# Two PSUM banks as two tensors instead of one, and V and w_in laid out by even and odd columns, in a fused attention and feed-forward kernel

## The chip, the core and the metric

The kernel runs on one core of a Trainium2 chip. A core has a matrix engine (PE in the profile, with its weight loads listed apart as PEld), a vector engine (DVE), a scalar engine (ACT), a general engine (POOL) and a queue engine (SP). Each works through its own list of instructions in order and waits on semaphores for the others. Matmul results go to PSUM, which has eight banks of 2 KB in each of 128 partitions; a bank holds 512 float32 values. The metric is device time in microseconds. The kernel before took 403.68 us, the median of three runs (402.3, 403.68 and 404.91).

## The reference, cut to what matters

Attention of 8 x 8 heads over 576 tokens with head dimension 64. A token sees the tokens within 32 of it; 8 global tokens see all and are seen by all. Its output, 4608 tokens of 512 features, goes through a feed-forward layer with weights w_in (512 x 2048) and w_out (2048 x 512).

```
scores = 0.125 * q @ k.T                          # per batch and head
mask   = (|i - j| <= 32) or i is global or j is global
attn   = softmax(where(mask, scores, -1e9))
x      = (attn @ v) as [4608 tokens, 8 heads * 64]
h      = x @ w_in
out    = (s * relu(h)**2 + b) @ w_out
```

## The kernel before, in words

Work on attention goes by pairs of heads: 32 pairs, four to a batch. For pair p the keys are cut in five chunks. `qk(p, c)` (L517) is one matmul of up to 384 columns into a tile `pss`, an exponential on ACT into `e` (L523), and a multiplication with the mask on DVE into `em` (L526). After every second pair `pvq` (L528) multiplies `em` by V, four heads side by side, each in its own 32 columns of the array. The stationary operand is a 32-column piece of `vring`, where V lies in bf16; `part` 0 is a column of ones for the sums, `part` 1 and 2 are the first and the second half of a head's 64 columns. Two steps of the normalisation follow (L590, L593) and DVE writes x, transposed, into `xt`, whose four slices of 128 partitions are pairs of heads and halves of their columns. The rows of `w_in` must lie in the same order; L164 and the four loads at L837 do that. Eight copies on POOL (L608, `scatter`) put the global tokens' columns into `xt` when a batch is done.

The feed-forward layer goes by tiles of 512 tokens, nine in all, 32 quanta each (`moe_quanta`, L616). Quantum f of the first 16 takes a bank, runs four matmuls of 512 columns over w_in into it (L631), and ACT evicts it with a ReLU into `r` (L638), which DVE squares into `g` (L641). The last 16 quanta are four banks of 16 matmuls over w_out (L650), which DVE evicts as `osb` or `osbh` (L670, L667). Each time a bank is taken is a turn; `bank` (L106) counts them.

Of the eight banks `ps_s` (for `pss` and some transposes) takes two, `ps_o` (for `po`) two, `ps_m` two, and `ps_x` holds one tile of two banks, named `spare` in the code and `psx` in the profile. In the first pairs `spare` is a second accumulator for `pvq` (blocks with `blk` 1, `m` below 2), and the place that the warming matmuls on zeros (`warm`, L780) write. After pair 4 `early` is false, and `bank` hands out in turn two tiles of `ps_m` (named `psh`, `pso`, `pst`, `psg`), then the first half of `spare`, then its second half, and so on: two turns in `ps_m`, two in `spare`. Whatever is written or read there is then named `psx`.

The order of every engine's instructions is the order of the code (a manual schedule); `later` holds steps that are put behind the next matmuls. Pairs 0 to 4 run alone (`first_pair`); from pair 5 on each of a pair's eight steps (`run_pair`) has one quantum of the feed-forward layer behind it, so that from about 50 us on the two kinds of work alternate, and from about 330 us on the last tiles run alone. The queue of POOL carries in order: the loads of k and q of pairs 1 to 3 (`load_kq`, L170, rounding to bf16 on the way), the gathers of the global rows, two of the four w_in loads, k and q of pair 4, the other two w_in loads, a cast of V, V of pair 4, and so on.

Of the kernel before, what the change touches and what calls it, by code (L numbers as in the profile page):

```python
# [9 lines left out]
FP32 = mybir.dt.float32  # L10
# [6 lines left out]
P = 128  # L17
# [3 lines left out]
DM, DF = 512, 2048  # L21
# [16 lines left out]
NVR = 5  # L38
# [7 lines left out]
DH = D // 2  # L46
# [13 lines left out]
def view(ap, *dims):  # L60

    return bass.AP(
        tensor=ap.tensor, offset=ap.offset, ap=[list(ap.ap[0])] + [list(d) for d in dims]
    )
# [3 lines left out]
def kernel(  # L68
# [12 lines left out]
    nc = tc.nc  # L81
# [15 lines left out]
    globp = ctx.enter_context(tc.tile_pool(name="globp", bufs=2))  # L97
    ps_s = ctx.enter_context(tc.tile_pool(name="ps_s", bufs=2, space=bass.MemoryType.PSUM))
    ps_o = ctx.enter_context(tc.tile_pool(name="ps_o", bufs=1, space=bass.MemoryType.PSUM))
    ps_x = ctx.enter_context(tc.tile_pool(name="ps_x", bufs=1, space=bass.MemoryType.PSUM))  # L100
    ps_m = ctx.enter_context(tc.tile_pool(name="ps_m", bufs=2, space=bass.MemoryType.PSUM))
    spare = ps_x.tile([P, 2 * DM], FP32, tag="x", name="psx")
    turns = [0]
    early = [True]

    def bank(name):  # L106

        turns[0] += 1
        if early[0] or turns[0] % 4 < 2:
            return ps_m.tile([P, DM], FP32, tag="moe", name=name)[:]  # L110
        return spare[:, DM * (turns[0] % 2) :][:, 0:DM]


    from concourse.hw_specs import get_activation_tables
# [25 lines left out]
    for t, eng in (("k", nc.sync), ("q", nc.scalar)):  # L140
        eng.dma_start(
            out=six0[t].rearrange("p (h x) -> p h x", h=2),
            in_=src[t][0, 0:2].rearrange("h (p j) d -> p h (j d)", j=NJ),
# [5 lines left out]
        out=gidx_p[:],  # L149
        in_=bass.AP(  # L150
            tensor=global_idx.tensor, offset=global_idx.offset, ap=[[0, P // NG], [1, NG], [1, 1]]
        ),
    )
    nc.scalar.dma_start(out=gidx_i64[:], in_=_bcast_dram(global_idx[:], P))
    vring = const.tile([P, NVR, NCH, 2, D], BF16)
    qbufs = [const.tile([P, 2, LQ], BF16, name=f"qbd{i}", tag=f"qbd{i}") for i in range(3)]
    gqd = [const.tile([P, 2, D], BF16, name=f"gqd{i}", tag=f"gqd{i}") for i in range(2)]
    win_t = wpool.tile([P, 4, DF], BF16)
# [2 lines left out]
    wsum = wpool.tile([P, DM], FP32)  # L161
    s_bc = const.tile([P, 1], FP32)
    b_bc = const.tile([P, 1], FP32)
    w_in2 = moe_w_in.rearrange("(g j h i) f -> j i g h f", g=2, j=4, h=2)  # L164
    w_out2 = moe_w_out.rearrange("(a p) n -> p a n", p=P)

    def load_kq(p):
        bi, hp = divmod(p, 4)
        for t in "kq":
            nc.gpsimd.dma_start(  # L170
                out=six[t][:NP6, p % NR].rearrange("p h j d -> p h (j d)"),
                in_=src[t][bi, 2 * hp : 2 * hp + 2].rearrange("h (p j) d -> p h (j d)", j=NJ),
            )
# [69 lines left out]
    def cast_v(eng, p):  # L243
# [4 lines left out]
            name=nc.get_next_instruction_name(), act_func_set_id=_set_id,  # L248
# [18 lines left out]
    for t in gqd:  # L267
# [21 lines left out]
    part = const.tile([P, 1], I32)  # L289
    nc.vector.tensor_scalar(  # L290
        out=part[:], in0=rowi[:], scalar1=3, scalar2=7,
# [5 lines left out]
        out=half[:], in0=partf[:], scalar=2.0 * S, in1=half[:], op0=OP.mult, op1=OP.add  # L297
    )
    nc.vector.tensor_copy(
        out=six["k"][:NP6, 0].rearrange("p h j d -> p (h j d)"), in_=six0["k"]  # L300
# [48 lines left out]
    for t in gadd:  # L349
# [7 lines left out]
        out=band[:], in0=band[:], scalar1=(float(WIN) + 0.5) ** 2, scalar2=None, op0=OP.is_le  # L357
# [25 lines left out]
    def flush():  # L383
        ops, later[:] = list(later), []
        for f in ops:
            f()

    def globals_of(bb):
# [9 lines left out]
        def turn():  # L398
            ps = bank("psg").bitcast(BF16)[:, 0 : 2 * D].rearrange("p (i d) -> p i d", i=2)
            for i in range(2):  # L400
                for hh in range(2):
                    r = slice(D * hh, D * hh + D)
                    nc.tensor.transpose(ps[r, i], gb[r, i], ident[r, r])

            def evac():
                eng = nc.vector.tensor_copy if bb else nc.scalar.copy
                eng(out=gkt[bb][:], in_=ps[:, 0])
                for hh in range(2):
                    r = slice(D * hh, D * hh + D)
                    eng(out=gqd[bb % 2][r, hh], in_=ps[r, 1])  # L410

            later.append(evac)
# [115 lines left out]
    def pvq(m, blk):  # L528

        po = spare if blk and m < 2 else ps_o.tile([P, 2 * DM], FP32, tag="o", name="po")  # L530
        otile[(m, blk)] = po
        x0, x1 = SPAN[blk]
        started = set()
        for part in range(3):
            for c in range(NCH):
                lo, hi = max(LO[c], x0), min(HI[c], x1)
                while lo < hi:
                    a = CUT * part + lo - x0
                    n = min(hi - lo, DM * (a // DM + 1) - a)
                    for j in range(4):  # L540
                        p, hh = 2 * m + j // 2, j % 2
                        key = (a // DM, j)
                        nc.tensor.matmul(  # L543
                            po[DH * j : DH * j + DH, a : a + n],
                            vring[:, p % NVR, c, hh, DH * (part - 1) : DH * part]
                            if part
                            else onesb[:],
                            emt[(p, c)][:, hh, lo - LO[c] : lo - LO[c] + n],
                            start=key not in started, stop=(part == 2),
                            skip_group_check=True,  # L550
                        )
                        started.add(key)
                    lo += n
# [127 lines left out]
    moe = moe_quanta()  # L681
# [18 lines left out]
    def put_out(m, blk):  # L700
        pvq(m, blk)
        pending.extend(norm_steps(m, blk))
# [48 lines left out]
            Q(nq[s])  # L751

    def idle_bank():
        return spare[:, 0:DM] if early[0] else bank("psw")

    def select(p):

# [22 lines left out]
    def warm(n):  # L780

        ps = idle_bank()
        for _ in range(n):
            nc.tensor.matmul(ps, dummy[:, 0:P], dummy[:])  # L784

    def first_pair(p, extra={}):
# [40 lines left out]
        out=sel6[:], in0=view(idx6[:], [1, NJ], [0, NG]),  # L827
# [5 lines left out]

    gather(0, "kqv")
    load_kq(3)
    for a in range(4):
        nc.gpsimd.dma_start(  # L837
            out=win_t[:, a], in_=w_in2[:, :, a // 2, a % 2]
        )
        if a == 1:  # L840
            load_kq(4)
    clear(qbufs[1][0:D, 1], LQ)
    clear(qbufs[1][D:P, 0], LQ)
# [5 lines left out]
        out=vkey[:], in0=kidx[:], scalar1=float(S) - 0.5, scalar2=None, op0=OP.is_le  # L849
    )  # L850
    for i in range(2):
        c = i * (NCH - 1)
        nc.vector.tensor_copy(
            out=gadd[i][:, GAP : GAP + NG], in_=view(vkey[:, c : c + 1], [0, NG])
# [3 lines left out]
        out=sel[:], in0=view(kidx[:], [1, NCH], [0, NG]),  # L858
# [42 lines left out]
        elif p == 2:  # L901
            load_kq(6)
    flush()
    early[0] = False
    warm(12)
    scatter(0)
    load_w_out(1)
# [1 line left out]
    for i in (1, 2, 3):  # L909
# [5 lines left out]
        out=view(natb[96:P], [DM, NV * NCH * P // DM], [1, DM]),  # L915
        in_=view(dummy[96:P], [0, NV * NCH * P // DM], [1, DM]),
    )
    nc.sync.dma_start(
        out=view(six["q"][96:P], [384, 10], [1, 384]), in_=view(dummy[96:P], [0, 10], [1, 384])
# [28 lines left out]
    for p in range(4, NPAIR):  # L948
# [18 lines left out]
        if p == 5:  # L967
            for i in range(NG):
                nc.gpsimd.dma_start(
                    out=gvall[i : i + 1].rearrange("o (b h d) -> o b h d", b=B - 2, h=H),  # L970
                    in_=v[2:, :, ds(greg_p[i], 1), :].rearrange("b h o d -> o b h d"),
# [6 lines left out]
        if p >= 6 and p + 2 < NPAIR:  # L978
# [4 lines left out]
            for i, j in enumerate(todo):  # L983
                if j < NPAIR:
                    x = 4 if p in (8, 9) else 4 * i
# [66 lines left out]
```

## Time and profile before

| | |
|---|---|
| median of three runs | 403.68 us |
| profiled execution: time, span of the core | 407.0 us, 405.3 us |
| PE busy | 352.4 us, 87% of the span, 3232 matmuls |
| DVE, ACT, POOL busy | 238.4, 226.1, 72.1 us |
| mean granted PE clock | 0.966 |
| ACT's evictions `r` from `psx`, from `psh` | 74 and 70 |
| HBM read, written | 42.20 MB, 9.44 MB |

The profile is of one execution, whose time is 3.3 us above the median. Times in rows count from the span's start. A row of the timeline gives start, length, engine, line, operation, output and input, and in brackets how long the engine stood idle before and what ended that. Matmuls overlap in the pipeline: a row's length of a lone matmul of 512 columns is longer than the step from one to the next.

### The profile page before, as it was taken

To read this page: it belongs to the slowest core of one execution; us is meant where nothing else is said; L and a number is where in the kernel's file an instruction comes from. 1 tells how busy PE (TensorE), PEld (TensorE's weight loads), DVE (VectorE), ACT (ScalarE), POOL (GpSimd) and SP (SyncE) were. 2 spreads that over 40 slices of the span, in tenths; PEclk is the share of its full clock that TensorE was granted. 3 is DMA by queue.
4 is the path that set the end of the run, shared out by engine and by line. 5 is a ranking of instruction groups with operands and counts; after the bars stand their busy time and mean duration, and the time that the engine had idled before them with its cause. 6 is when DMAs were issued, how large, how long until landed. Compare 5 with 4: busy or idle time off the path is not lost.

```text
span 405.3 us, 8660 instructions
## 1 busy us (share of the span) xinstructions
PE 352.4 (87%) x3232; PEld 178.0 (44%) x3232; DVE 238.4 (59%) x677; ACT 226.1 (56%) x454; POOL 72.1 (18%) x151
## 2 busy tenths in 40 slices
PE   7773889898999799988988889898989898899896
PEld 3341444454444244556643434344446543344344
DVE  6663656866868379776665566766665643322421
ACT  6661657655885377756773676667656623502510
POOL 7824484206001201050002000300020010000000
PEclk9995798999999699999998999999999999999999
DMA  6999799999979677859157924882430011011002
GB/s 133 180 154 151 117 173 224 173 188 229 179 133 196 120 179 146 212 116 193 46 136 190 221 62 121 203 184 45 137 96 29 2 53 53 2 53 53 0 27 78
DMA packets 122197, 50.51 MB, mean 125 GB/s; under 512 B 108819, under 2 KB 115635, under 8 KB 122155
## 3 DMA queue, kind: packets, MB, share of 16 engines
q1 hardware_dynamic: 112058, 37.49, 43.4%
q0 software_dynamic: 9600, 12.04, 17.0%
q8 instruction: 25, 0.41, 0.4%
q10 hardware_dynamic: 496, 0.43, 0.4%
q14 instruction: 18, 0.14, 0.1%
HBM read 42.20 MB, written 9.44 MB: 127 GB/s over the span
## 4 chain that ended last, share of the span: by engine, by line
issue 40%; PE 37%; POOL 6%; DMA 5%; ACT 5%; DVE 4%; SPq 1%; POOLq 0%; ACTq 0%
PE psx L631 9%; PE psh L631 8%; PE pso L650 7%; PE psx L650 7%; DMA sixq<-in_q_dram 5%; ACT r L638 3%; POOL xt L608 3%; PE po L543 2%; PE pss L519 2%; POOL gf L319 2%; PE psx L784 1%; PE pst L472 1%; DVE xt L584 1%; POOL vring L244 1%; DVE osb L670 1%
## 5 line engine op out<-in xcount | busy, mean ns | idle before, releaser
L523 ACT ACTIVATE e<-pss 128x384 bf16<-128x384 f32 (+1 forms) x160 | 74.5, 470 | 55.6 <-PE pss L519 52.3
L631 PEld LDWEIGHTS <-win_t 128*128 128x128 bf16 x704 | 65.1, 99 | 87.6 <-issue 38.3
L641 DVE TENSOR_TENSOR g<-r 128x512 bf16<-128x512 bf16 x144 | 59.8, 422 | 67.5 <-ACT r L638 65.5
L631 PE MATMUL psx<-xt,win_t 128*128 128x512 bf16 (+2 forms) x364 | 77.9, 345 | 23.9 <-ACT r L638 20.5
L650 PEld LDWEIGHTS <-g 128*128 128x128 bf16 x592 | 56.5, 98 | 67.3 <-issue 10.0
L650 PE MATMUL pso<-wout_t,g 128*128 128x512 bf16 (+1 forms) x320 | 73.6, 369 | 0.0
L631 PE MATMUL psh<-xt,win_t 128*128 128x512 bf16 (+2 forms) x340 | 72.2, 349 | 1.5 <-POOL xt L608 1.5
L526 DVE TENSOR_TENSOR em<-e,mask 128x384 bf16<-128x384 bf16 (+1 forms) x160 | 55.8, 349 | 30.1 <-ACT e L523 29.9
L638 ACT ACTIVATE r<-psx 128x512 bf16<-128x512 f32 x74 | 44.4, 600 | 50.4 <-PE psx L631 45.5
L650 PE MATMUL psx<-wout_t,g 128*128 128x512 bf16 x272 | 66.6, 387 | 6.5 <-DVE osb L670 6.0
L638 ACT ACTIVATE r<-psh 128x512 bf16<-128x512 f32 x70 | 42.0, 599 | 41.5 <-PE psh L631 40.4
L519 PE MATMUL pss<-qbd,kt 128*128 128x384 bf16 (+1 forms) x160 | 53.0, 340 | 2.8 <-DVE qbd L447 1.6
L608 POOL COPY xt<-xg 128x4 bf16 x64 | 17.3, 270 | 167.9 <-DVE xt L584 164.4
L519 PEld LDWEIGHTS <-kt 128*128 128x128 bf16 x160 | 16.1, 102 | 21.7 <-DVE qbd L447 4.1
L584 DVE TENSOR_TENSOR xt<-po,rep 128x120 bf16<-128x120 f32 (+1 forms) x60 | 25.1, 459 | 0.5 <-ACT rep L594 0.5
L501 DVE COPY qbd<-pst 64x600 bf16<-64x600 bf16 x38 | 17.8, 468 | 11.6 <-PE pst L459 11.1
L506 DVE COPY qbd<-pst 64x600 bf16<-64x600 bf16 x20 | 15.6, 778 | 14.1 <-ACT qbd L506 8.1
L670 DVE SCALAR_TENSOR_TENSOR osb<-psx,s_bc,bias_row 128x512 f32<-128x512 f32 x12 | 9.0, 746 | 18.3 <-PE psx L650 18.3
L543 PE MATMUL po<-em,vring 128*32 128x160 bf16 (+2 forms) x896 | 18.3, 221 | 0.1
L201 ACT CAST natb<-natk 120x640 bf16<-120x640 f32 x24 | 17.4, 726 | 0.0
L784 PE MATMUL psx<-dummy 128*128 128x512 bf16 x33 | 14.0, 535 | 3.4 <-DVE xt L584 2.0
L929 POOL DMA_DIRECT2D wst<-in_moe_w_out_dram x8 | 5.8, 731 | 60.7 <-DVE wsum L933 34.2
(121 smaller groups left out, 289.2 us busy)
## 6 DMA issues: line engine op xcount, KB each, us to landing
natv<-in_v_dram SPq DMA_DIRECT2D x55, 150.0 KB
natk<-in_k_dram SPq DMA_DIRECT2D x47, 150.0 KB
out_dram<-osb SPq DMA_DIRECT2D x23, 256.0 KB
natq<-in_q_dram SPq DMA_DIRECT2D x37, 150.0 KB
wst<-in_moe_w_out_dram POOLq DMA_DIRECT2D x8, 512.0 KB, 5.2
out_dram<-osbh SPq DMA_DIRECT2D x9, 256.0 KB
win_t<-in_moe_w_in_dram POOLq DMA_DIRECT2D x4, 512.0 KB, 19.7
wout_t<-in_moe_w_out_dram POOLq DMA_DIRECT2D x4, 512.0 KB, 9.1
```

What stands on the lines that cost most here:

```text
L501: eng(out=view(qbufs[p % 3][r, hh], [P, NCH], [HB + NG, 2], [1, HB]), in_=view(ps[r], [P, NCH], [HB, 2], [1, HB]),)
L519: nc.tensor.matmul(ps[:], ktile[p][:, P * c : P * c + P], qbufs[p % 3][:, :, LO[c] : HI[c]])
L523: nc.scalar.activation(e[:], ps[:], AF.Exp, scale=SCALE)
L526: later.append(lambda: nc.vector.tensor_mul(em[:], e[:], masks[c]))
L543: nc.tensor.matmul(po[DH * j : DH * j + DH, a : a + n], vring[:, p % NVR, c, hh, DH * (part - 1) : DH * part] if part else onesb[:], emt[( ...
L584: nc.vector.tensor_tensor(out=view(xt[:, 2 * g, x0 + t0 :], [NXT, 2], [w, runs], [1, w]), in0=view(po[:, CUT + col :], [CUT, 2], [P, runs] ...
L608: nc.gpsimd.tensor_copy(out=xt[:, :, S * (bi % NX) : S * (bi % NX) + S][:, :, ds(greg_p[i], 1)], in_=xgs[bi][:, :, i : i + 1],)
L631: nc.tensor.matmul(psh[:, d0 : d0 + n], win_t[:, a, f * P : f * P + P], xt[:, a, x0 : x0 + n], start=(a == 0 and j == 0), stop=(a == 3), s ...
L638: nc.scalar.activation(r[:], psh, AF.Relu)
L641: later.append(lambda g=g, r=r: nc.vector.tensor_mul(g[:], r[:], r[:]))
L650: nc.tensor.matmul(pso[:, 0:nn], gl[f][:, u * P : u * P + P], wout_t[:, f, n0 : n0 + nn], start=(f == 0), stop=(f == 15),)
L784: nc.tensor.matmul(ps, dummy[:, 0:P], dummy[:])
```

## The change

Three edits. First, `ps_x` with its tile `spare` is opened in a stack of its own, which is closed after pair 4, and a pool `ps_n` with two one-bank tiles takes its place; `bank` takes two turns from `ps_m`, then two from `ps_n`. The turn numbers and so the banks stay the same, but each turn's tile is now a tensor of its own. Second, `part` 1 and 2 of V are the even and the odd columns of a head, so that the stationary operand is read with a step of two elements. Third, `w_in` is ordered to match: partition p of slice (g, h) holds row 256 g + 2 p + h, so a partition's two rows for one g lie side by side in memory. The four loads are now by halves of the 2048 columns (outer) and by g (inner), each of 128 partitions x 2 rows x 1024 columns, where each was one slice of 128 partitions x 2048 columns. The pair-4 load stays between the second and the third.

```diff
--- before.py
+++ after.py
@@ -97,18 +97,18 @@
     globp = ctx.enter_context(tc.tile_pool(name="globp", bufs=2))
     ps_s = ctx.enter_context(tc.tile_pool(name="ps_s", bufs=2, space=bass.MemoryType.PSUM))
     ps_o = ctx.enter_context(tc.tile_pool(name="ps_o", bufs=1, space=bass.MemoryType.PSUM))
-    ps_x = ctx.enter_context(tc.tile_pool(name="ps_x", bufs=1, space=bass.MemoryType.PSUM))
     ps_m = ctx.enter_context(tc.tile_pool(name="ps_m", bufs=2, space=bass.MemoryType.PSUM))
+    first = ctx.enter_context(ExitStack())
+    ps_x = first.enter_context(tc.tile_pool(name="ps_x", bufs=1, space=bass.MemoryType.PSUM))
     spare = ps_x.tile([P, 2 * DM], FP32, tag="x", name="psx")
     turns = [0]
-    early = [True]
+    rings = [ps_m]
 
     def bank(name):
 
         turns[0] += 1
-        if early[0] or turns[0] % 4 < 2:
-            return ps_m.tile([P, DM], FP32, tag="moe", name=name)[:]
-        return spare[:, DM * (turns[0] % 2) :][:, 0:DM]
+        pool = rings[turns[0] // 2 % len(rings)]
+        return pool.tile([P, DM], FP32, tag="moe", name=name)[:]
 
 
     from concourse.hw_specs import get_activation_tables
@@ -161,7 +161,7 @@
     wsum = wpool.tile([P, DM], FP32)
     s_bc = const.tile([P, 1], FP32)
     b_bc = const.tile([P, 1], FP32)
-    w_in2 = moe_w_in.rearrange("(g j h i) f -> j i g h f", g=2, j=4, h=2)
+    w_in2 = moe_w_in.rearrange("(g p h) f -> p g h f", g=2, h=2)
     w_out2 = moe_w_out.rearrange("(a p) n -> p a n", p=P)
 
     def load_kq(p):
@@ -542,7 +542,7 @@
                         key = (a // DM, j)
                         nc.tensor.matmul(
                             po[DH * j : DH * j + DH, a : a + n],
-                            vring[:, p % NVR, c, hh, DH * (part - 1) : DH * part]
+                            view(vring[:, p % NVR, c, hh, part - 1 :], [2, DH])
                             if part
                             else onesb[:],
                             emt[(p, c)][:, hh, lo - LO[c] : lo - LO[c] + n],
@@ -751,7 +751,7 @@
             Q(nq[s])
 
     def idle_bank():
-        return spare[:, 0:DM] if early[0] else bank("psw")
+        return spare[:, 0:DM] if len(rings) == 1 else bank("psw")
 
     def select(p):
 
@@ -833,11 +833,11 @@
 
     gather(0, "kqv")
     load_kq(3)
-    for a in range(4):
-        nc.gpsimd.dma_start(
-            out=win_t[:, a], in_=w_in2[:, :, a // 2, a % 2]
-        )
-        if a == 1:
+    for j in range(2):
+        x = slice(1024 * j, 1024 * j + 1024)
+        for g in range(2):
+            nc.gpsimd.dma_start(out=win_t[:, 2 * g : 2 * g + 2, x], in_=w_in2[:, g, :, x])
+        if j == 0:
             load_kq(4)
     clear(qbufs[1][0:D, 1], LQ)
     clear(qbufs[1][D:P, 0], LQ)
@@ -901,7 +901,8 @@
         elif p == 2:
             load_kq(6)
     flush()
-    early[0] = False
+    first.close()
+    rings.append(ctx.enter_context(tc.tile_pool(name="ps_n", bufs=2, space=bass.MemoryType.PSUM)))
     warm(12)
     scatter(0)
     load_w_out(1)
```

On every engine the instructions stand in the same order as before; names of tiles, waits and the shape of the four loads differ.

PE, the first quanta of tile 7, in the last stage without attention, before (`psx_102` is `spare`; a number after a name is one tensor):

```order
L631 MATMUL psx_102<-xt_108,win_t_122 128x512
L631 LDWEIGHTS win_t_122
L631 MATMUL psx_102<-xt_108,win_t_122 128x512 [waits Activation_49]
...
L631 LDWEIGHTS win_t_122
L631 MATMUL psh_5688<-xt_108,win_t_122 128x512
...
L631 MATMUL psx_102<-xt_108,win_t_122 128x512 [waits Activation_49]
...
L631 MATMUL psx_102<-xt_108,win_t_122 128x512 [waits Activation_49]
```

And the same places now:

```order
L631 MATMUL psh_5741<-xt_108,win_t_122 128x512
L631 LDWEIGHTS win_t_122
L631 MATMUL psh_5750<-xt_108,win_t_122 128x512 [waits DVE_49]
...
L631 LDWEIGHTS win_t_122
L631 MATMUL psh_5768<-xt_108,win_t_122 128x512 [waits Activation_49]
...
L631 MATMUL psh_5777<-xt_108,win_t_122 128x512 [waits Activation_49]
...
L631 MATMUL psh_5786<-xt_108,win_t_122 128x512 [waits Activation_49]
```

No matmul moved. Before, all turns in `spare` write one tensor, and the wait of the third row is for ACT's read of the other half, which the matmuls directly ahead of it have just filled. Now every turn has its own tensor, and the wait at a turn's first matmul is for the reader of the same bank four turns back.

POOL, the loads around w_in, as one piece of the difference:

```order
 L170 DMA sixk<-in_k_dram 96x2x384
 L170 DMA sixq<-in_q_dram 96x2x384 [waits DMASW0_49]
-L837 DMA win_t<-in_moe_w_in_dram 128x1x2048 [waits DMASW1_49]
-L837 DMA win_t<-in_moe_w_in_dram 128x1x2048 [waits DMASW2_49]
+L839 DMA win_t<-in_moe_w_in_dram 128x2x1024 [waits DMASW1_49]
+L839 DMA win_t<-in_moe_w_in_dram 128x2x1024 [waits DMASW2_49]
 L170 DMA sixk<-in_k_dram 96x2x384 [waits DMASW3_49]
 L170 DMA sixq<-in_q_dram 96x2x384 [waits DMASW4_49]
-L837 DMA win_t<-in_moe_w_in_dram 128x1x2048 [waits DMASW5_49]
-L837 DMA win_t<-in_moe_w_in_dram 128x1x2048 [waits DMASW6_49]
+L839 DMA win_t<-in_moe_w_in_dram 128x2x1024 [waits DMASW5_49]
+L839 DMA win_t<-in_moe_w_in_dram 128x2x1024 [waits DMASW6_49]
```

The first two rows are k and q of pair 3, the middle two are k and q of pair 4. Order and waits stay; what each w_in load carries changes. The source of a load before was four groups of 32 rows by stride (`j` and `i` of L164), and is now 128 partitions of one stride.

## Rows read from the trace of the kernel before

**Rows 1.** What PE waited for, whole span: us in total, times, longest us

```profile
PE psx L631 <- ACT r L638: 20.5, 33, 1.3
PE pst L472 <- DMA sixq<-in_q_dram: 6.1, 1, 6.1
PE psx L650 <- DVE osb L670: 6.0, 5, 2.6
...
PE pss L519 <- DVE qbd L447: 1.6, 3, 0.7
...
PE psx L631 <- DVE osbh L667: 1.2, 1, 1.2
```

**Rows 2.** Timeline of PE, last stage: start us, us, what, [idle before]

```profile
340.24 1.02 PE L631 MATMUL psx<-xt,win_t 128*128 128x512 bf16 x4 [0.69 <-ACT r L638]
341.10 1.89 PE L631 MATMUL psh<-xt,win_t 128*128 128x512 bf16 x8
...
344.54 1.02 PE L631 MATMUL psx<-xt,win_t 128*128 128x512 bf16 x4 [0.69 <-ACT r L638]
```

**Rows 3.** Timeline of PE in the middle stage, beside attention

```profile
94.79 0.33 PE L519 MATMUL pss<-qbd,kt 128*128 128x384 bf16 x1
95.64 1.02 PE L631 MATMUL psx<-xt,win_t 128*128 128x512 bf16 x4 [0.52 <-ACT r L638]
```

**Rows 4.** Timeline of PE, after two of the longer waits

```profile
62.02 3.49 PE L631 MATMUL psh<-xt,win_t 128*128 128x512 bf16 x8
...
214.10 1.02 PE L650 MATMUL psx<-wout_t,g 128*128 128x512 bf16 x4 [2.57 <-DVE osb L670]
...
215.25 4.44 PE L650 MATMUL psx<-wout_t,g 128*128 128x512 bf16 x12
```

**Rows 5.** Stretches: length, busy us of each engine, PEclk, DMA share, GB/s

```profile
36.00:45.00 9.00, 7.39 (x112) 3.72 (x108) 5.04 (x16) 4.28 (x10) 2.70 (x4) 0.51 1.20 171
214.00:219.50 5.50, 5.39 (x21) 2.26 (x21) 1.99 (x7) 0.00 (x0) 1.92 (x7) 0.69 0.62 209
...
219.66:240.41 20.75, 18.16 (x170) 8.76 (x168) 13.60 (x41) 13.84 (x29) 0.00 (x0) 1.00 0.78 164
```

**Rows 6.** Timeline at the start of tile 3: POOL's copies and PE's first matmul

```profile
173.05 3.50 POOL L608 COPY xt<-xg 128x4 bf16 x8 [5.65 <-DVE xt L584]
...
176.94 1.03 PE L631 MATMUL psx<-xt,win_t 128*128 128x192 bf16 x8 [1.17 <-DVE osbh L667]
```

**Rows 7.** Timeline of PE and ACT, pairs 3 and 4

```profile
29.08 0.30 PE L519 MATMUL pss<-qbd,kt 128*128 128x320 bf16 x1 [0.44 <-ACT e L523]
...
30.24 0.49 ACT L594 ACTIVATE rep<-ln 128x316 f32<-128x316 f32 x1
...
35.43 0.69 PE L472 MATMUL pst<-ident,sixq 96*64 96x96 bf16 x12 [6.05 <-DMA sixq<-in_q_dram]
...
36.17 0.66 ACT L506 COPY qbd<-pst 64x600 bf16<-64x600 bf16 x1 [5.44 <-PE pst L472]
```

**Rows 8.** Timeline of POOL: the loads as it issues them

```profile
14.10 1.44 POOL L837 DMA_DIRECT2D win_t<-in_moe_w_in_dram  x2
...
16.18 0.67 POOL L170 DMA_DIRECT2D sixq<-in_q_dram  x1
...
32.45 0.69 POOL L170 DMA_DIRECT2D sixk<-in_k_dram  x1 [7.18 <-DMA win_t<-in_moe_w_in_dram]
```

**Rows 9.** DMA packets by size, from 22 to 29 and from 29 to 33 us

```profile
DMA packets 384, 1.11 MB, mean 159 GB/s; under 512 B 98, under 2 KB 116, under 8 KB 384
...
DMA packets 939, 0.65 MB, mean 162 GB/s; under 512 B 631, under 2 KB 823, under 8 KB 938
```

**Rows 10.** Small stationary operands: loads by tile (ns min/median/max), and two timeline rows

```profile
L543 PEld LDWEIGHTS <-vring x960: 92/97/151, 25.9 to 330.3; 128*32 128x32 bf16 x192
...
56.75 0.45 PE L472 MATMUL pst<-ident,sixk 96*64 96x96 bf16 x12
...
57.33 0.57 PE L543 MATMUL po<-em,vring 128*32 128x160 bf16 x28
```

## The prediction

> **What bounds the kernel now.** The page first: PE is busy 87% of the span, the next engine, DVE, 238.4 of 405.3 us or 59%, so the question is what keeps PE from its matmuls. The list of PE's waits answers it [rows 1]. One wait leads: a matmul into `psx` waits for ACT's ReLU `r`, 33 times, 20.5 us. Then come one wait of 6.1 us for k and q of pair 4, and five of together 6.0 us for DVE's eviction `osb`. The waits for `psh`, the same work in the other two banks, do not occur. Next the timeline of the last stage, where nothing but the feed-forward layer runs [rows 2]. Four turns make a period of 344.54 - 340.24 = 4.30 us. Four matmuls take 341.10 - 340.24 = 0.86 us, so sixteen need 3.44 us and 0.86 us is lost in every period, at one place: the second of the two turns in `spare`. It waits for the eviction of the first, which writes another bank. The two halves are one tensor, so the wait is taken for the whole of it. In the middle stage the same gap stands between `pss` and `psx` [rows 3]. Then the first pairs: PE stands from 29.4 to 35.43 us [rows 7], and the stretch behind it runs at a granted clock of 0.51 [rows 5].
>
> **a. ACT's read of the other half.** The change gives every turn its own tensor, so a turn's first matmul waits for the reader of the same bank four turns back. The twelve matmuls of the three turns between take 12 x 0.215 = 2.6 us alone, and longer beside attention, while an eviction is through within 0.7 us [rows 2]. Each of the 33 waits should go. One is worth more than its row says: 0.86 us are lost where 0.69 are shown, because the pipeline fills again. Gain 20.5 + 33 x 0.17 = 26.1 us. All of it lies on the path: PE is the engine that sets the end, and no other one becomes the bound, since a tile's busiest stretch has PE at 18.2 of 20.75 us, ACT at 13.8 and DVE at 13.6 [rows 5]. With four such waits out (20.75 - 4 x 0.85 = 17.4 us), ACT and DVE stand at 80%.
>
> **b. DVE's read of the other half.** The same with `osb` and `osbh`: 6.0 + 1.2 us and six refills of 0.17, 8.2 us [rows 1]. At tile 3 something else is late next: PE starts there at 176.94 behind `osbh`, but POOL's copies into `xt`, which tile 3 reads, end at 173.05 + 3.50 = 176.55 [rows 6]. So 0.4 of the 1.2 us is kept, and b is 7.4 us.
>
> **c. The clock behind two of these waits.** The eight matmuls at 62.02 take 3.49 us, against 1.89 for eight at full clock [rows 2, 4], and the twelve at 215.25 take 4.44 against 12 x 0.215 + 0.17 = 2.75. The stretch around the latter has a granted clock of 0.69 [rows 5]; PE had stood 2.57 us for `osb` just before. Without the waits I take both falls away: 1.6 + 1.7 = 3.3 us, with 0 as the other end.
>
> **d. k and q of pair 4.** POOL issues two w_in loads, then these two, then two more of w_in [rows 8]. Issued at 16.18, q lands only as PE starts at 35.43, 19 us later. Packets tell why: from 22 to 29 us nearly all that is not a semaphore write is w_in (268 packets of over 2 KB; 116 - 98 = 18 of k and q, which are 768 B); from 29 to 33 us 823 - 631 = 192 of k and q come [rows 9]. So a part of q stood behind w_in on some DMA engines until these had done whole w_in loads, all four loads running at once. If each load is spread evenly over the DMA engines instead, only the two ahead of it delay q: 1.05 MB in bf16 at the 159 GB/s of that stretch is 6.6 us, q and k 0.29 MB or 1.9 us. The first data moves at about 17.4 us (issue ends at 15.5, and 0.29 MB of pair 3 are ahead), so pair 4 is there at 17.4 + 6.6 + 1.9 = 26 us, 3 us ahead of its use. Then ACT, which is free at 30.24 + 0.49 = 30.73, starts `qbd` 5.4 us earlier than at 36.17 [rows 7]. I take 5.4; the ends are 0 and the 6.1 of the wait.
>
> [...]
>
> Behind d the stretch from 36 to 45 us runs at half clock with PE busy 7.4 of 9 us [rows 5]. If the clock stays up, up to 3 us more are won, fewer because ACT and DVE then lead; I take 1.
>
> **e. New waits.** Today DVE's `qbd` is late at three pair starts, by 0.7 us at most [rows 1]; with 0.5 to 0.7 us less before it PE meets it oftener. Between 0 and 0.7 at each of six tile starts, 4 us; I take 2.
>
> **f. V by even and odd columns.** 960 stationary loads of 32 columns read with a step of two elements. Loads take 97 ns and hide behind other matmuls: 28 V matmuls with their loads take 0.57 us, 20 ns each [rows 10]. If a load over a span of 64 columns paced like the transposes, which load 64 (12 in 0.45 us, 38 ns), it would cost 18 x 960 ns = 17 us. Below, a gain has no source: the same columns and matmuls. I take 0, since the matmul's own 92 to 192 columns set the pace, and keep 17. [...] No row of this trace has such a load. w_in's loads on POOL stay four instructions; their order and what queues behind them is the same, and k of pair 5 and a cast of V, which stood behind w_in until 32.45 [rows 8], come earlier. The warming matmuls take the new bank behind the last reader of `spare`, as now.
>
> **The sum**: 26.1 + 7.4 + 3.3 + 5.4 + 1 - 2 = 41.2 us off 407.0, the profiled execution, is 365.8. That execution is 3.3 us above the median of 403.68, so the runs should show 403.7 - 41.2 = 362.5, and I say 362.
>
> **The rivals.**
> - *w_in in smaller packets is no quicker.* If a 2 KB packet takes as long as a 4 KB one, the two loads need 13.2 us, pair 4 lands at 32.5, and d gives about 3 and no clock: 403.7 - 37.8 = 366; if q is as late as now, 369. Against it, packets of 768 B move at a like rate [rows 9].
> - *The step costs V's loads.* Up to 17 us: 362.5 to 379.5. It decides the size, not the sign.
> - *The banks still wait.* If a pool of two tiles made a turn wait for the turn ahead, a, b and most of c stay, and d alone gives 6.4: 397. Against it, the banks of `ps_m` are such a pool and have no such wait in rows 1.
> - *Slower: V's loads no longer hide at all.* PE would stand for every one of 960 loads. At a full 97 ns less the 20 it takes now, 74 us, less the gain: 403.7 - 41.2 + 74 = 436. It decides from 41.2 us / 960 = 43 ns a load. For it speaks only that no such load was seen; against it, loads of 32 columns run ahead of the matmuls today, and PE has room in its list.
>
> **How the numbers follow.** Chances: forecast 0.75 (357 to 367, the spread of c, d and e); small packets 0.1 (366 to 369); V's loads in part 0.08 (365 to 379); banks still wait 0.03 (397); V's loads in full 0.03 (436); gains eaten by something unseen 0.01. The low end is all ends together: 26.1 + 8.2 + 3.3 + 6.1 + 3 = 46.7, or 357, and 1 us for the spread of runs. The high end is the first rival with c gone and e at 4 (26.1 + 7.4 + 0 + 0 - 4 = 29.5), 374. That leaves out the upper half of V's case and the last three. What a measurement here tells from no change is 1%, 4 us: faster 0.95, same 0.02, slower 0.03.
>
> **What would show it.** After: no wait of PE for `r` or `osb` at a turn's start, periods of 3.45 us in the last stage (a, b); tile 3 starting right behind POOL's copies (b); full clock around tile 0's eighth quantum and at tile 3's end (c); `pst` of pair 4 by 30 us, with the two w_in loads ahead of it landed by 25 (d); 28 V matmuls in 0.57 us still (f). It is wrong if PE waits for `em`, `qbd` or `pss` by more than 5 us in sum, if V's row grows, or if the tail's period stays at 4.30.

## The result, and the profile after

The changed kernel takes 366.45 us, median of four runs (365.62 to 367.5), against 403.74 us before (402.3 to 404.91). The ratio is 0.908, with a 95% interval of 0.904 to 0.912. The profiled execution takes 366.32 us, span 364.6 us, at a mean granted clock of 0.991. It is 40.7 us shorter than the profiled execution of before.

PE's waits over the whole span, as in [rows 1]: us in total, times, longest us.

```profile
PE psh L631 <- POOL xt L608: 5.3, 5, 2.2
PE psx L784 <- DVE xt L584: 2.9, 1, 2.9
PE psg L403 <- DVE gb L396: 2.9, 2, 1.8
PE pss L519 <- ACT e L523: 2.3, 4, 1.1
PE pss L519 <- DVE qbd L447: 2.0, 4, 0.7
...
PE po L543 <- DVE xt L584: 0.6, 1, 0.6
```

No wait for `r`, `osb` or `osbh` is left, and none for q of pair 4. What leads now is POOL's copies of the global columns into `xt`, at five tile starts; three of these waits were there before.

PE's timeline of the changed kernel, in the order of the prediction: pairs 3 and 4, beside attention, the start of tile 3, and the last stage, with one row of ACT there.

```profile
29.22 0.45 PE L472 MATMUL pst<-ident,sixq 96*64 96x96 bf16 x12
...
43.58 2.75 PE L631 MATMUL psh<-xt,win_t 128*128 128x512 bf16 x12
...
87.81 0.33 PE L519 MATMUL pss<-qbd,kt 128*128 128x384 bf16 x1
87.97 1.03 PE L631 MATMUL psh<-xt,win_t 128*128 128x512 bf16 x4
...
91.32 0.57 PE L543 MATMUL po<-em,vring 128*32 128x160 bf16 x28
...
162.18 0.95 PE L631 MATMUL psh<-xt,win_t 128*128 128x320 bf16 x7 [0.76 <-POOL xt L608]
...
305.77 13.98 PE L631 MATMUL psh<-xt,win_t 128*128 128x512 bf16 x63
...
307.70 0.60 ACT L638 ACTIVATE r<-psh 128x512 bf16<-128x512 f32 x1 [0.27 <-PE psh L631]
...
319.58 5.78 PE L650 MATMUL pso<-wout_t,g 128*128 128x512 bf16 x25
```

The first row is the transposes of q of pair 4, which stood at 35.43 [rows 7]. The feed-forward matmuls at 87.97 follow `pss` with no gap, where [rows 3] had 0.52 us. In the last stage sixteen turns run as one block from 305.77 to 319.58: 13.81 us, or 3.45 for four turns, against 4.30 [rows 2]. ACT evicts a bank in 0.60 us meanwhile (at 307.70 the second of the block), and PE fills the next one without a gap. The V matmuls take 0.57 us as before [rows 10].

The stretches with the granted clock of the changed kernel (columns as in [rows 5]), then its DMA packets from 22 to 29 us, as the first row of [rows 9]:

```profile
34.50:38.00 3.50, 3.50 (x88) 2.25 (x87) 1.49 (x5) 1.80 (x5) 1.23 (x2) 0.51 1.23 191
68.50:72.50 4.00, 4.00 (x13) 1.58 (x12) 0.82 (x5) 0.75 (x2) 0.72 (x1) 0.57 1.45 213
72.50:363.00 290.50, 278.78 (x2530) 146.75 (x2565) 188.87 (x518) 177.61 (x362) 31.16 (x75) 1.00 0.67 129
```

```profile
DMA packets 1062, 1.53 MB, mean 219 GB/s; under 512 B 123, under 2 KB 491, under 8 KB 1061
```

PE runs at half clock twice, for some 3.5 us each: behind the wait of 2.90 us for `xt` and behind one of 1.81 for `gb`. From 72.5 us on it keeps full clock. From 22 to 29 us all DMA together moves 219 GB/s where it moved 159 [rows 9].

### The profile page after: what moved, and what is told of

It reads as the page before. It is cut to its first block, busy times and chain, and to the rows that moved or that the text cites. A ratio compares the mean times of both kernels' runs of the same rounds, so it can differ in the third digit from the quotient of the medians.

```text
span 364.6 us, 8611 instructions
## 1 busy us (share of the span) xinstructions
PE 336.0 (92%) x3187; PEld 175.6 (48%) x3232; DVE 238.7 (65%) x677; ACT 224.1 (61%) x454; POOL 74.1 (20%) x151
## 4 chain that ended last, share of the span: by engine, by line
PE 48%; issue 27%; DVE 9%; DMA 8%; POOL 4%; ACT 3%; POOLq 0%; SPq 0%; DVEq 0%
PE psh L631 21%; PE pso L650 17%; PE po L543 3%; PE pss L519 3%; DMA natk<-in_k_dram 2%; POOL xt L608 2%; DVE xt L584 2%; DMA wst<-in_moe_w_out_dram 2%; DMA gf<-in_q_dram,grow 2%; DVE qbd L506 1%; DMA out_dram<-osb 1%; ACT e L523 1%; DVE em L526 1%; PE pst L472 1%; POOL gf L319 1%
## 5 line engine op out<-in xcount | busy, mean ns | idle before, releaser
L631 PE MATMUL psh<-xt,win_t 128*128 128x512 bf16 (+4 forms) x687 | 136.3, 339 | 6.0 <-POOL xt L608 5.3
L650 PE MATMUL pso<-wout_t,g 128*128 128x512 bf16 (+1 forms) x569 | 134.8, 376 | 2.2 <-issue 1.6
L638 ACT ACTIVATE r<-psh 128x512 bf16<-128x512 f32 x144 | 86.6, 602 | 62.5 <-PE psh L631 57.4
L631 PEld LDWEIGHTS <-win_t 128*128 128x128 bf16 x704 | 64.0, 98 | 60.2 <-issue 7.0
L608 POOL COPY xt<-xg 128x4 bf16 x64 | 18.1, 284 | 149.1 <-DVE xt L584 145.5
L670 DVE SCALAR_TENSOR_TENSOR osb<-pso,s_bc,bias_row 128x512 f32<-128x512 f32 (+1 forms) x25 | 18.1, 724 | 26.3 <-PE pso L650 26.3
L591 ACT ACTIVATE ln<-po 128x324 f32<-128x324 f32 (+1 forms) x30 | 13.1, 438 | 3.9 <-PE po L543 3.9
L594 ACT ACTIVATE rep<-ln 128x324 f32<-128x324 f32 (+1 forms) x32 | 15.3, 479 | 0.1
L543 PEld LDWEIGHTS <-vring 128*32 128x32 bf16 x960 | 14.8, 101 | 0.0
L244 ACT CAST vring<-natv 128x640 bf16<-128x640 f32 x20 | 14.4, 724 | 0.2 <-DMA natv<-in_v_dram 0.2
## 6 DMA issues: line engine op xcount, KB each, us to landing
win_t<-in_moe_w_in_dram POOLq DMA_DIRECT2D x4, 512.0 KB, 11.3
```

The costliest lines, as they stand in the source:

```text
L543: nc.tensor.matmul(po[DH * j : DH * j + DH, a : a + n], view(vring[:, p % NVR, c, hh, part - 1 :], [2, DH]) if part else onesb[:], emt[(p, ...
L608: nc.gpsimd.tensor_copy(out=xt[:, :, S * (bi % NX) : S * (bi % NX) + S][:, :, ds(greg_p[i], 1)], in_=xgs[bi][:, :, i : i + 1],)
L631: nc.tensor.matmul(psh[:, d0 : d0 + n], win_t[:, a, f * P : f * P + P], xt[:, a, x0 : x0 + n], start=(a == 0 and j == 0), stop=(a == 3), s ...
L638: nc.scalar.activation(r[:], psh, AF.Relu)
L650: nc.tensor.matmul(pso[:, 0:nn], gl[f][:, u * P : u * P + P], wout_t[:, f, n0 : n0 + nn], start=(f == 0), stop=(f == 15),)
L670: nc.vector.scalar_tensor_tensor(out=osb[:, 0:nn], in0=pso[:, 0:nn], scalar=s_bc[:], in1=bias_row[:, n0 : n0 + nn], op0=OP.mult, op1=OP.add,)
```

## The experiments

Each time is a median and stands beside runs of the kernel before on the same chip (medians 405 to 406 there).

**1. The banks alone, 2. the layout alone.** The first takes the change of `bank`, `spare` and `ps_n` and leaves V and w_in; the second is the change with the old `bank` put back.

```diff
 # 1, on the kernel before; 2 is the reverse of it on the changed kernel
-        if early[0] or turns[0] % 4 < 2:
-            return ps_m.tile([P, DM], FP32, tag="moe", name=name)[:]
-        return spare[:, DM * (turns[0] % 2) :][:, 0:DM]
+        pool = rings[turns[0] // 2 % len(rings)]
+        return pool.tile([P, DM], FP32, tag="moe", name=name)[:]
...
-    early[0] = False
+    first.close()
+    rings.append(ctx.enter_context(tc.tile_pool(name="ps_n", bufs=2, space=bass.MemoryType.PSUM)))
```

> The banks alone: two one-bank tensors after pair 4; V in halves and the four w_in loads as before. Theory (the false waits and the w_in loads add up, and share nothing): the 39 waits for r, osb and osbh go as they did in the change, the 6 us wait of PE for q of pair 4 stays, with the stretch at half clock behind it; 403.7 less the 30 to 32 us that the change won behind 50 us = 372 to 374. Rival (part of the gain behind 50 us comes from V or from w_in landing earlier): 376 or more, with waits of PE for em, qbd or w_in that the change does not have.

> The layout alone: V by even and odd columns, w_in in four loads of 128 x 2 x 1024, and the one two-bank tensor as before. Theory: PE does not wait for q of pair 4, the 33 waits for r stay; 6 us off, 397 to 398. Rival one (the step of two elements costs in V's loads, and the banks hid it): above 399 with V's matmuls longer than 0.57 us for 28. Rival two (an earlier w_in lets other work come earlier too): below 395.

Measured: the banks alone 372.03 us, ratio 0.922 (0.914 to 0.930); the layout alone 398.83 us, ratio 0.987 (0.982 to 0.992). Their product is 0.910, and the change itself has 0.908 and, run again, 0.906. So the parts add up, and the banks bring some five sixths of it. The two leading rows of PE's waits, of the banks alone and of the layout alone:

```profile
PE pst L472 <- DMA sixq<-in_q_dram: 8.4, 2, 8.2
PE psh L631 <- POOL xt L608: 5.3, 5, 2.1
```

```profile
PE psx L631 <- ACT r L638: 22.0, 33, 2.8
PE psx L650 <- DVE osb L670: 6.0, 5, 2.6
```

Each has the waits that the other one lost.

**3. The two-bank tensor kept, the turns in another order.**

```diff
-        if early[0] or turns[0] % 4 < 2:
+        if early[0] or turns[0] % 2:
             return ps_m.tile([P, DM], FP32, tag="moe", name=name)[:]
-        return spare[:, DM * (turns[0] % 2) :][:, 0:DM]
+        return spare[:, DM * (turns[0] // 2 % 2) :][:, 0:DM]
```

> The two-bank tensor is kept, and so are V and w_in of before; only the turn order changes: one turn in a bank of ps_m, one in a half of the tensor, and so on, so that the reader of the other half belongs to the turn two back, with four matmuls (0.86 us) between its matmuls and the waiting one. Theory (what cost the time is the wait for a whole tensor directly after it was filled): nearly all of the waits for r go, 374 to 378, while waits for osb stay in part. Rival (PE cannot fill one half while ACT reads the other, or these two banks are slow): the waits stay, 400 or more.

Measured: 376.15 us, ratio 0.932 (0.924 to 0.940), as the theory had it. Of PE's waits two for `r` are left, 2.8 us, and none for `osb`, where some had been expected. PE's timeline of this kernel, middle and last stage:

```profile
68.45 1.86 PE L631 MATMUL psx<-xt,win_t 128*128 128x512 bf16 x4 [2.43 <-ACT r L638]
...
330.43 1.03 PE L631 MATMUL psh<-xt,win_t 128*128 128x512 bf16 x4
331.29 1.03 PE L631 MATMUL psx<-xt,win_t 128*128 128x512 bf16 x4
```

In the last stage each turn follows the one ahead by 0.86 us, in the same two banks and the same tensor. So the banks are not slow: it was the wait for the whole tensor, and a turn in between covers it. This kernel still waits for the reader of the other half before it writes, so it does not show whether PE could write one half while ACT reads the other; the block without a gap in the last stage of the changed kernel does. The turn in between covers the wait only while ACT is on time; at 68.45 ACT was late, PE stood 2.43 us, and the four matmuls behind that took 1.86 us, against 1.03 in the last stage, which I take for a fallen clock. By the medians this kernel is 4 us behind the banks alone, but the two intervals overlap (0.924 to 0.940 and 0.914 to 0.930).

**4. k and q of pair 4 ahead of all w_in loads**, on the kernel before. This tests my reason for the late q by itself.

```diff
+    load_kq(4)
     for a in range(4):
         nc.gpsimd.dma_start(
             out=win_t[:, a], in_=w_in2[:, :, a // 2, a % 2]
         )
-        if a == 1:
-            load_kq(4)
```

> The kernel before with one move: k and q of pair 4 are issued on POOL ahead of all four w_in loads, whose shape stays. Theory (q of pair 4 was late because w_in packets stood ahead of it): PE's wait of 6 us is gone, pair 4 starts at about 30 us and 6 us come off, 397 to 398, as far as w_in is there by the first feed-forward matmul. Rival (the w_in loads in their old shape take so long that the first feed-forward matmul at 44 us, or V of pair 4, waits instead): 400 to 404.

Measured: 404.68 us, ratio 1.002 (0.998 to 1.007): nothing won. PE's wait for q of pair 4 goes, as the theory said, but the time is nearly the rival's 400 to 404, though neither w_in nor V of pair 4 is what PE then waits for. PE's timeline of this kernel, then its packets from 22 to 29 us:

```profile
28.01 0.45 PE L472 MATMUL pst<-ident,sixq 96*64 96x96 bf16 x12
...
38.72 0.94 PE L543 MATMUL po<-em,vring 128*32 128x160 bf16 x26 [3.57 <-DMA vring<-gvx]
...
44.45 0.45 PE L472 MATMUL pst<-ident,sixq 96*64 96x96 bf16 x12 [1.92 <-DMA sixq<-in_q_dram]
...
50.46 1.02 PE L631 MATMUL psx<-xt,win_t 128*128 128x512 bf16 x4 [0.62 <-POOL xt L608]
```

```profile
DMA packets 218, 0.82 MB, mean 118 GB/s; under 512 B 18, under 2 KB 18, under 8 KB 218
```

q of pair 4 is there at 28 us, but a w_in load takes 23.8 us from issue to landing (median), and all DMA of that stretch together moves 118 GB/s. A small write into `vring` from SP's queue (10.0 KB) holds PE until 38.72, q of pair 5, issued at 24.96, until 44.45, and the first feed-forward matmul comes at 50.46, no earlier than before (49.99). Taking one load out from behind w_in is not enough; the next experiment asks what a faster w_in does.

**5. and 6. The source of a load against the size of its packets.** The fifth kernel is the change with w_in in whole rows again (4 KB packets), from 128 rows of one stride. The sixth has 2 KB packets, but from four groups of 32 rows, as before, with V in halves to match; this takes eight loads in place of four.

```diff
 # 5
...
-            nc.gpsimd.dma_start(out=win_t[:, 2 * g : 2 * g + 2, x], in_=w_in2[:, g, :, x])
...
+        nc.gpsimd.dma_start(out=win_t[:, a], in_=w_in2[:, a // 2, a % 2])
 # 6
-    w_in2 = moe_w_in.rearrange("(g p h) f -> p g h f", g=2, h=2)
+    w_in2 = moe_w_in.rearrange("(g j h i) f -> j i g h f", g=2, j=4, h=2)
...
-            nc.gpsimd.dma_start(out=win_t[:, 2 * g : 2 * g + 2, x], in_=w_in2[:, g, :, x])
+                nc.gpsimd.dma_start(out=win_t[:, a + h, x], in_=w_in2[:, :, a // 2, h, x])
```

> The change, with w_in loaded as four slices of 128 partitions x 2048 columns: packets of 4 KB as before, but the source is 128 rows of one stride, no longer four groups of 32. Theory (what makes q of pair 4 come early is that a load is spread evenly over the DMA engines, whatever the packet): no wait of PE for q, 366 to 368, and from 22 to 29 us about 200 GB/s. Rival (the halved packets do it, since a packet of pair 4 waits for a shorter one ahead): the wait of 6 to 8 us is back, 371 to 374.

> The change, with V in halves and the rows of w_in as before, w_in loaded in eight loads of 128 x 1024: packets of 2 KB as in the change, but the source is four groups of 32 rows as before. POOL issues four loads more, two of them (1.4 us) ahead of k and q of pair 4. Theory (the spread decides): q is late again, PE waits 6 to 9 us, 371 to 375. Rival (the small packets decide): no wait over 1 us, 366 to 368. V has no step here: V's rows must read 0.57 us for 28 matmuls as in the change.

Measured: the fifth 367.05 us, ratio 0.902 (0.895 to 0.908), as the change; the sixth 373.26 us, ratio 0.919 (0.912 to 0.926), as the banks alone. Packets from 22 to 29 us of the fifth, then of the sixth:

```profile
DMA packets 805, 1.51 MB, mean 216 GB/s; under 512 B 127, under 2 KB 508, under 8 KB 805
```

```profile
DMA packets 2249, 0.98 MB, mean 140 GB/s; under 512 B 1532, under 2 KB 1916, under 8 KB 2249
```

With sources in four groups all DMA of that stretch moved 140 GB/s with packets of 2 KB here, 118 and 159 with 4 KB (experiment 4 and [rows 9]); with sources in 128 rows 216 and 219. These rates count everything that was under way, also k and q (packets of 768 B). By the packets of 2 KB and over, w_in itself had an estimated 97, 117 and 157 GB/s of them with four groups, 174 and 167 with 128 rows. The fifth kernel is the clean one: with the old size of packet and the new source it is as fast as the change, so the halved packets, which the change names, decide nothing here. The sixth kernel's loss did not stand where I expected it, at q. From its timeline of PE and POOL:

```profile
27.35 0.73 POOL L244 CAST vring<-natv 128x640 bf16<-128x640 f32 x1
...
28.65 0.79 PE L543 MATMUL po<-em,vring 128*32 128x160 bf16 x26 [2.87 <-DVE vring L436]
...
47.61 2.75 PE L631 MATMUL psh<-xt,win_t 128*128 128x512 bf16 x12
```

PE waits 2.87 us for a piece of `vring`, and its first feed-forward matmul comes 4 us behind that of the change (43.58). That piece follows POOL's cast of V at 27.35 us, which the change has at 18.58: POOL stood 1.85, 1.27 and 2.71 us between issues of the eight loads, until earlier loads had landed. The time came out by the theory, the wait did not, and how much of the loss is the source and how much the four loads more is not separated.

**7. V's operand with a step of eight elements** in place of two. It reads other columns of V, so its values are not the reference's.

```diff
-                            view(vring[:, p % NVR, c, hh, part - 1 :], [2, DH])
+                            view(vring[:, p % NVR, min(c, NCH - 2), 0, part - 1 :], [8, DH])
```

> The change, with V's stationary operand read with a step of eight elements (16 bytes) where the change has two; it reads other columns of V than the reference wants, so the values are not the reference's. Theory (a load of 32 columns hides behind other matmuls at any step): 28 V matmuls in 0.57 us, 366 to 368. [...]

Measured: 370.17 us, ratio 0.906 (0.898 to 0.914), which is not told apart from the change. The rows are clearer: 28 V matmuls take 0.64 us, so the theory's 0.57 did not hold. The loads of `vring` and one group of V matmuls, of the changed kernel and then of this one (loads: ns min/median/max):

```profile
L543 PEld LDWEIGHTS <-vring x960: 93/97/151, 25.7 to 298.6; 128*32 128x32 bf16 x192
...
97.01 0.58 PE L543 MATMUL po<-em,vring 128*32 128x92 bf16 x32
```

```profile
L543 PEld LDWEIGHTS <-vring x960: 134/155/170, 25.6 to 303.5; 128*32 128x32 bf16 x192
...
51.18 0.64 PE L543 MATMUL po<-em,vring 128*32 128x160 bf16 x28
...
98.11 0.70 PE L543 MATMUL po<-em,vring 128*32 128x92 bf16 x32
```

A load takes 155 ns in place of 97, and 0.07 to 0.12 us of it show in each of the 32 groups, an estimated 3 us in sum. At a step of two a load takes the 97 ns that it took without one, at a step of eight 58 ns more. Steps between these were not run, and why the one is slower, no run shows.

**8. Half of the copies into `xt` on ACT, 9. all of them.** The profile after points at these waits.

```diff
 # 9; 8 does the same for odd i alone. ACT loads its registers greg_a as POOL does greg_p
-            nc.gpsimd.tensor_copy(
-                out=xt[:, :, S * (bi % NX) : S * (bi % NX) + S][:, :, ds(greg_p[i], 1)],
+            nc.scalar.copy(
+                out=xt[:, :, S * (bi % NX) : S * (bi % NX) + S][:, :, ds(greg_a[i], 1)],
...
```

> The change, with the eight copies of the global columns into xt shared: four on POOL as now, four on ACT. The changed kernel shows five waits of PE for POOL's copies, 5.3 us, each at a tile's start, the eight copies taking 2.9 to 3.5 us there. Theory: with four copies a side POOL is done 1.5 us earlier; four waits of 0.7 to 0.84 us go, the one of 2.15 falls to 0.9; with a refill of 0.17 each 5 us off, 361 to 363. Rival (ACT's copies hold up the ReLU and the exponentials behind them, or each side waits for the other's copies since both write one xt): 366 or more.

> The change, with all eight copies of the global columns on ACT, so that no copy waits for one on another engine. Where they were shared, each copy waited 0.30 us for the one before it on the other engine, four pairs took 2.1 us, and four waits of together 4.0 us stayed. Theory (the handing over cost it, and ACT has nothing else to do there): copies back to back, eight in 1.7 to 2 us, beginning right behind DVE's last product, not behind POOL's load that waits for wsum; the five waits of 5.3 us and their refills of 0.17 go, 360 to 361. Rival (ACT's exponential behind the copies is late and PE waits for em in place of xt): 365 or more.

Measured: shared, 365.93 us, ratio 0.902 (0.894 to 0.910), no faster than the change. All on ACT, 360.84 us, ratio 0.889 (0.884 to 0.893), against 367.06 and 0.906 (0.901 to 0.911) of the change run beside it. The copies of tile 2 in the timeline, shared:

```profile
122.24 0.74 POOL L937 DMA_DIRECT2D wst<-in_moe_w_out_dram  x1 [4.78 <-DVE wsum L941]
122.97 0.41 POOL L609 COPY xt<-xg 128x4 bf16 x1
123.41 0.21 ACT L609 COPY xt<-xg 128x4 bf16 x1 [3.52 <-POOL xt L609]
123.68 0.20 POOL L609 COPY xt<-xg 128x4 bf16 x1 [0.30 <-ACT xt L609]
123.92 0.21 ACT L609 COPY xt<-xg 128x4 bf16 x1 [0.30 <-POOL xt L609]
```

All on ACT, and last the copies of tile 4 of the changed kernel, on POOL:

```profile
119.08 1.91 ACT L608 COPY xt<-xg 128x4 bf16 x8 [0.75 <-DVE xt L584]
...
122.26 0.31 PE L519 MATMUL pss<-qbd,kt 128*128 128x320 bf16 x1 [1.33 <-ACT sixq L225]
```

```profile
196.38 2.92 POOL L608 COPY xt<-xg 128x4 bf16 x8 [30.99 <-DVE xt L584]
```

It is the change's own lesson again: eight writes to other columns of one tensor are put in a row, whichever engine makes them. Of the 0.30 us in brackets 0.20 or 0.21 is the other engine's copy, and some 0.05 is left for each of the two changes of engine. So a shared pair takes 123.92 - 123.41 = 0.51 us, as much as two copies in a row on one engine (1.91 / 4 = 0.48 on ACT), and sharing wins nothing. All on ACT wins by two other things: the eight take 1.91 us, at 44.27 us 1.89, where POOL takes 2.92 at tile 4, and at tile 2 they begin at 119.08, behind DVE's last product, where on POOL they stand behind the load at 122.24. PE's waits for `xt` at the tile starts are gone. The first feed-forward matmul of this kernel comes at 46.21 us, against 43.19 of the change beside it; why, no run shows.

**10. The transposes of `gb` one step later, 11. both, 12. the change beside them.**

```diff
             elif p % 8 == 7:
-                at(1, steps[1])
+                at(2, steps[1])
```

> The change itself once more, beside the next three: 366 to 367, with the five waits for POOL's copies (5.3 us), the wait of 1.8 us for the rounded global rows gb at 68 us, and half clock just behind that.

> The change, with the transposes of the rounded global rows gb one step later in every pair that has them (step 2 in place of 1). Theory (PE waits there because DVE's cast stands behind three squares; one matmul step later it is done, and the clock fell at 68.7 us because PE had stood): the wait of 1.8 us goes, no half clock from 68.7 to 72.1 us, 1.8 + 0.17 + 1.7 = 3.7 us off the change, 362.5 to 363.5. Rival one (the clock falls there whatever PE waits for): 364.5, half clock still near 70 us. Rival two (the wait passes to the next step, for qbd or kt made from these rows): 366.

> Both of the last two: the copies on ACT and the transposes one step later. Theory (the two are apart in time and add up): 6 + 3.7 us off the change, 356 to 357.5. Rival (what one gives back the other loses, since DVE, with the squares and qbd, then sets the pace at the tile starts): 359 or more, with waits for qbd or em grown by 2 us or more.

Measured: the change again 367.06 us; one step later 366.29 us, ratio 0.900 (0.895 to 0.904), not told apart from it; both 359.05 us, ratio 0.883 (0.880 to 0.887), the lowest median of all, but not told apart from all copies on ACT alone. Both forecasts missed: 362.5 to 363.5 for the tenth, 356 to 357.5 for the eleventh. The change run again shows why the tenth won so little. Its stretches around 70 and behind 124.9 us:

```profile
68.00:73.00 5.00, 4.77 (x63) 2.52 (x65) 2.68 (x9) 2.89 (x7) 0.72 (x1) 1.00 1.18 187
124.90:128.30 3.40, 3.38 (x9) 1.20 (x9) 1.48 (x4) 1.92 (x4) 0.00 (x0) 0.50 1.23 241
```

In this execution the wait for `gb` was 1.28 us and the clock held; it fell behind the wait of 1.97 us for POOL's copies. So there was no half clock at 70 us to win back; my expectation for the tenth kernel had taken it from one execution. In the tenth the wait for `gb` went to 0.26 us, while one for `e` ahead of it grew from 1.60 to 1.91.

## Why the prediction was right, and where it was off

The forecast was 362 us and the measured median 366.45, inside the forecast's 357 to 367 but at its upper end. The cause is the one that was named.

**a and b** went as worked out. All 33 waits for `r` and all for `osb` and `osbh` are gone, and the last stage runs at 3.45 us a period. Tile 3 starts behind POOL's copies, which end at 158.63 + 3.50 = 162.13 us, and waits 0.76 us for them: the order of who is late next was read rightly from [rows 6].

```profile
158.63 3.50 POOL L608 COPY xt<-xg 128x4 bf16 x8 [4.61 <-DVE xt L584]
```

**d** had the right size and an incomplete mechanism. Forecast were 5.4 us and 1 more for the clock; the first feed-forward matmul comes 49.99 - 43.58 = 6.41 us earlier. But I kept the rate of 159 GB/s and laid the delay to what stood ahead of q. Experiment 4 puts q first and wins nothing; experiment 5 shows that the source of 128 rows pays whatever the packets. A w_in load then lands 11.3 us after its issue (13.7 in experiment 5), where it took 19.7 before and 23.8 in experiment 4, so that not q alone comes earlier: POOL issues the first load of w_out, which stands behind w_in, at 28.40 us in place of 36.57. The loads of before and of the changed kernel, KB each and median us from issue to landing:

```profile
win_t<-in_moe_w_in_dram POOLq DMA_DIRECT2D x4, 512.0 KB, 19.7
...
win_t<-in_moe_w_in_dram POOLq DMA_DIRECT2D x4, 512.0 KB, 11.3
```

Which DMA engines a load used, and what the packets under 512 B were, no row shows. That a part of q stood behind w_in on some of the engines, and that the new source spreads each load evenly over them, was my estimate, and the 5.4 us and the landing at 26 us rest on it. What the runs show in its place is the time to landing, 11.3 us against 19.7, the transposes of q at 29.22 us in place of 35.43, and the 6.41 us.

**e** was too small. I took 2 us. The rows for POOL's copies grew from 2.2 + 1.5 to 5.3, `gb` by 0.4, `e` from 1.0 to 2.3, `qbd` from 1.6 to 2.0, and one wait of 0.6 for `xt` is new, 4.3 us in all. Of these 0.76 are tile 3's, which b had counted as staying; that leaves 3.5 against 2.

**c** and the base of the sum are where it went off. I tied two falls of the clock to two waits, at 3.3 us. Both are gone in either trace of the change, but each trace has another one: at 68.7 us in one, behind the wait for `gb`, and at 124.9 in the other, behind the wait for POOL's copies at tile 2. Before, there was a fall at that same tile start, at 133.5 us, which I had not counted. So the terms of one execution are not those of the next, and the same holds for the sum's base. I took 41.2 us, worked out from the profiled execution of before (407.0), off the median of 403.7. Between the two profiled executions 40.7 us were won, 6.4 up to the first feed-forward matmul and 34.3 behind it, where a + b + c - e had said 34.8. That they agree so closely is in part luck: e was 1.5 us too small, and the clock gave more than c (below). Between the medians it is 37.3. In the profiled execution of before three stretches behind 50 us are at half clock:

```profile
61.80:65.20 3.40, 3.40 (x10) 1.23 (x9) 2.98 (x11) 1.73 (x4) 1.64 (x3) 0.50 1.16 238
133.50:140.30 6.80, 5.45 (x14) 1.87 (x14) 1.48 (x4) 1.96 (x4) 1.32 (x4) 0.50 0.64 133
215.40:218.80 3.40, 3.40 (x10) 1.21 (x8) 1.94 (x6) 0.00 (x0) 0.82 (x2) 0.50 0.47 178
```

That is 13.6 us, where the changed kernel has 3.4: up to 5.1 us of time between these two, against 3.3 in c. The layout alone, which has the same banks and much the same waits behind 50 us (33 for `r`, 22.0 us against 20.5), has two such stretches:

```profile
127.60:131.00 3.40, 2.88 (x8) 0.99 (x7) 1.02 (x3) 1.83 (x4) 0.00 (x0) 0.50 0.78 122
206.10:209.50 3.40, 3.40 (x13) 1.33 (x10) 1.94 (x6) 0.00 (x0) 0.97 (x3) 0.50 0.51 194
```

That is 6.8 us. Half of the difference of 6.8 is 3.4 us, as much as the profiled execution was above its median. That the clock made up those 3.3 us fits, but is not shown: no other execution of that kernel has a trace. The mean granted clock, which is known of every execution, does not decide it: it was 0.966 in the profiled one, and on another chip five executions of the same kernel at 0.962 had spans from 399.1 to 404.6 us. So the cause of the 3.3 us stays open. If it was the clock, the sum should have been made without the half clock of that one execution, and would have come to about 366.

**f** held: a load takes 97 ns with the step as without, and the groups 0.57 and 0.58 us. Of the rivals, smaller packets as a brake fell to experiment 5, banks that still wait to the rows, and V's loads in part or in full to experiment 7, where even a slow load costs an estimated 3 us in all, not 17 or 74.

## What to carry to other kernels

Look in the list of waits for an engine that waits for the reader of something it does not overwrite: here the tensor is tracked as a whole (39 waits for `r`, `osb` and `osbh`, 27.7 us), and a split into tensors of its own, which left none of them, or another turn in between, which left two for `r` of together 2.8 us, gives the wait back. Before reordering a queue, ask whether what stands ahead is slow by its own shape: a load of 512 KB from 128 rows of one stride landed 11.3 to 13.7 us after its issue, one from four groups of 32 rows 19.7 to 23.8. And take a sum off the execution that it was worked out from; what its granted clock did there is not a property of the kernel.

## What had not been expected of the hardware

- With w_in from four groups of 32 rows all DMA together moved 118 to 159 GB/s from 22 to 29 us, with w_in from 128 rows of one stride 216 to 219, with packets of 2 KB as with 4 KB.
- Copies of 0.20 us that alternate between POOL and ACT on one tensor ran one at a time, 0.51 us a pair, so that four a side (124.92 + 0.21 - 122.97 = 2.16 us) were no faster than eight on ACT alone (1.91 us).
- A stationary load of 32 columns at a step of eight bf16 elements took 155 ns, at a step of two 97 ns as without a step.
- Where the clock falls is not fixed by the kernel: the same program fell to half behind a wait of 1.81 us at 68 us in one execution, and in another held there behind one of 1.28 us and fell behind one of 1.97 us at 124 us.
